# Dividing the first batch's heads by their row sums after the value product

## The chip, the core and the metric

The kernel runs on one core of a Trainium2 chip. The core has five engines with queues of their own: PE (matrix products, out of SBUF into the eight banks of PSUM), DVE and ACT (elementwise work, both read PSUM), POOL (elementwise work on SBUF alone) and SP (which issues the DMAs here). They meet only through semaphores. The metric is the time of one execution in device microseconds, as the median of several; the profile shows one such execution.

## The reference

Three layers stand behind one another: causal attention with a decay bias, a gated MLP, and a routed mixture of experts. The change touches only the end of the attention:

```
scores = scale * q @ k.T                       # 4 batches, 8 heads, 576 tokens, head_dim 64
scores = where(causal, -1e9, scores + minimum(bias, 0))
attn   = exp(scores - max(scores, axis=-1))
attn   = attn / (sum(attn, axis=-1) + 1e-9)    # row sums, one for each query
out    = attn @ v                              # what the MLP and the experts read
```

The division may stand before the product with v, on 576 x 576 exponentials of a head, or behind it, on 576 x 64 outputs.

## The kernel before

There are 32 heads (g = 0 to 31), and two heads make a pair. A head is worked in five blocks of query rows (i = 0 to 4: four of 128 rows, one of 64), block i against the 128 (i + 1) keys that the causal mask leaves it. `A_steps` walks heads and blocks in order and holds back what comes behind a block's scores by four blocks, so that the scores of one head are made while the head before it is finished:

- `emit_S(g, i)`: PE multiplies queries and keys into a PSUM bank (through the helper `mm3`, line 711); DVE adds the mask, takes the negated row maximum and writes the scores to the tile E (L409); ACT turns E into exponentials in place and adds up each row into column i of the tile `lsum` (L417). POOL adds 1e-9 (L421), DVE takes the reciprocal (L422), and POOL multiplies the rows of E by it, in place (L425).
- `emit_T(g, i)`: PE transposes E (L443) into a bank, and ACT or DVE copies that to `eta` (blocks 0 and 1) or `etb` (blocks 2 to 4), with keys on the partitions (L448, L450).
- `emit_PV(g, u)`: PE multiplies the values with `eta` (u = 0, 256 queries) or `etb` (u = 1, 320 queries) (L475). The output has head_dim on 64 partitions and the queries along the columns. ACT copies it to the tile `XF` of the pair (L487).
- `emit_X(p)`: PE transposes `XF` of a finished pair for a store (L504), and POOL splits it in two parts for the MLP (L498, L499).

The first batch (g < F4 = 8) uses plain float32 for exponentials and values; a float32 product stands in the trace as two instructions. In its time nothing of the MLP can run on PE yet. What runs beside it are the preparation of the MLP's weights (`split_f64`, lines 593 to 600, on ACT, DVE and POOL), the cumulated bias (`emit_cum`, lines 226 to 235, on DVE), the transposes of queries and keys for later heads (L334 on PE; lines 340 to 344 on ACT and DVE), and `warm_up` products, which compute nothing that is used (L166). The later batches run side by side with the MLP of the batch ahead of them.

PSUM has seven banks in rotation for all of this (`ps`, in the program's order), so a bank is free again when the engine that reads it has done so. A scheduler sets the order of the instructions on each engine; every engine then works strictly through its queue. Queries and keys of a head are put together by DMAs (`prep_asm`) from a single tile `tst`, which is written anew for the next pair.

Of the kernel before, what the change touches and what calls it, by code (L numbers as in the profile page):

```python
# [13 lines left out]
ALU = mybir.AluOpType  # L14
# [10 lines left out]
def f32v(ap):  # L25
    return ap.bitcast(F32)
# [7 lines left out]
def kernel(  # L34
# [19 lines left out]
    PE, ACT, DVE, POOL, SP = nc.tensor, nc.scalar, nc.vector, nc.gpsimd, nc.sync  # L54
# [7 lines left out]
    NQ = (S + 127) // 128  # L62
    QM = [min(128, S - 128 * i) for i in range(NQ)]
# [31 lines left out]
    def ps(tag="ps", bufs=7):  # L95
        t = psum.tile([128, 512], F32, tag=tag, name=tag, bufs=bufs)
        return t
# [18 lines left out]
    def T(pool, shape, dt, tag, bufs=1):  # L116
        _n[0] += 1
        return pool.tile(shape, dt, tag=tag, name=f"{tag}_{_n[0]}", bufs=bufs)

    ident = T(const, [128, 128], F32, "ident")  # L120
# [266 lines left out]
    Et, lsum, hred = {}, {}, {}  # L387

    def emit_S(g, i):
        qk = QK[buf[g]] if g >= ND else None  # L390
        M = QM[i]
        N = 128 * i + M
        e = T(ap_, [128, 128 * (i + 1)], F32, f"E{i}", bufs=2 if i==0 else 1) if i < NQ - 1 else E4
        Et[g, i] = e
        nm = T(ap_, [128, 2], F32, "negm", bufs=6)
        halves = [(0, N)] if N <= 512 else [(0, HS), (HS, N)]
        for hi, (a, z) in enumerate(halves):
            pt = ps()
            n = z - a
            qs = slice(128 * i, 128 * i + M)  # L400
            if g < ND:
                t = Tst[g // 2][64 * (g % 2):64 * (g % 2) + 64]
                r = slice(32 * g, 32 * g + 2 * NQ)
                pairs = [(t[:, 0, qs], t[:, 1, a:z]), (t[:, 0, qs], t[:, 3, a:z]), (t[:, 2, qs], t[:, 1, a:z]), (sel[r, qs], cumr[r, a:z])]
            else:
                pairs = [(qk[:, 0, qs], qk[:, 1, a:z]), (qk[0:KX, 2, qs], qk[0:KX, 3, a:z])]
            mm3(pt[0:M, 0:n], pairs, True, True)
            m0 = 512 - 128 * i + a if z == N else 0
            hred[g] = DVE.tensor_tensor_reduce(  # L409
                out=e[0:M, a:z], in0=pt[0:M, 0:n], in1=zmask[0:M, m0:m0 + n], scale=-1.0,  # L410
                scalar=BIG if hi == 0 else nm[0:M, 0:1], op0=ALU.add, op1=ALU.min, accum_out=nm[0:M, hi:hi + 1],
            )
        last = len(halves) - 1
        if i == 0:
            lsum[g] = T(ap_, [128, 8], F32, "lsum", bufs=3)
        l = lsum[g]
        ACT.activation(out=e[0:M, 0:N], in_=e[0:M, 0:N], func=ACTF.Exp, scale=-1.0, bias=nm[0:M, last:last + 1], accum_out=l[0:M, i:i + 1])  # L417
        if i in LG:
            i0 = LG[i]
            c = slice(i0, i + 1)  # L420
            POOL.tensor_scalar(out=l[0:M, c], in0=l[0:M, c], scalar1=1e-9, scalar2=0.0, op0=ALU.add, op1=ALU.add)  # L421
            DVE.reciprocal(out=l[0:M, c], in_=l[0:M, c])  # L422
            for x in range(i0, i + 1):
                n = 128 * x + M
                POOL.tensor_scalar(out=Et[g, x][0:M, 0:n], in0=Et[g, x][0:M, 0:n], scalar1=l[0:M, x:x + 1], scalar2=1.0, op0=ALU.mult, op1=ALU.mult)  # L425

    ET = {}
    LG = {z: z for z in range(NQ)}
# [26 lines left out]
    XH, XL, XF = {}, {}, {}  # L455

    def emit_PV(g, u):
        p, r = divmod(g, 2)
        vv = VV[g]
        et = ET.pop((g, u))  # L460
        q0, n = ((0, QA), (QA, QB))[u]
        pt = ps()
        js = range(2) if u == 0 else range(NQ)
        wide = g >= X3
        for j in js:
            kk = 128
            a = max(0, 128 * j - q0)
            if g < F4:
                ms = [(f32v(vv[0:kk, j, 0, :]), 0)]
            elif wide:  # L470
                ms = [(vv[0:kk, j, :, :].rearrange("p a d -> p (a d)"), z) for z in range(2)]
            else:
                ms = [(vv[0:kk, j, 0, :], 0), (vv[0:kk, j, 0, :], 1), (vv[0:kk, j, 1, :], 0)]
            for n_, (l, z) in enumerate(ms):
                PE.matmul(  # L475
                    pt[0:128 if wide else 64, a:n], lhsT=l, rhs=et[0:kk, z, j, a:n] if g >= F4 else f32v(et[0:kk, 0, j, a:n]),
                    start=(j == 0 and n_ == 0), stop=(j == js[-1] and n_ == len(ms) - 1),
                )
        if r == 0 and u == 0:
            XF[p] = T(ap_, [128, S], F32, "xf", bufs=2)  # L480
        po = 64 * r
        if wide:
            xc = T(ap_, [128, QB], F32, "xc")
            ACT.copy(out=xc[po:po + 64, 0:n], in_=pt[64:128, 0:n])
            DVE.tensor_tensor(out=XF[p][po:po + 64, q0:q0 + n], in0=pt[0:64, 0:n], in1=xc[po:po + 64, 0:n], op=ALU.add)
        else:
            ACT.copy(out=XF[p][po:po + 64, q0:q0 + n], in_=pt[0:64, 0:n])  # L487

    X3 = 12
    F4, TA = 8, (1, 3)  # L490
# [29 lines left out]
    def A_steps(LAG):  # L520
        fifo = []
        for n in range(NH * NQ):
            g, i = n // NQ, n % NQ
            p = g // 2
            if i == 0:
                for x in when:
                    if when[x] == g and g:
                        prep_asm(x)
            if g < len(WU) and WU[g]:
                warm_up(WU[g])  # L530
            emit_S(g, i)
            if (g, i) == EC0:
                emit_cum()
            yield 2 * max(107, (128 * i + QM[i]) * 0.42)
            fifo.append((g, i))
            if (g, i) == RS:
                prep_T(1, 0)
                prep_T(1, 1)
                prep_load(2)
                for x in when:  # L540
                    if when[x] == 0:
                        prep_asm(x)
            for p in range(1, NH // 2):
                if (when.get(2 * p) or g) - 1 == g and i in (3, 4):
                    prep_T(p, i - 3)
                    if i == 4 and p + 1 < NH // 2:
                        prep_load(p + 1)
                    yield 600
            if len(fifo) > LAG:
                yield from after(*fifo.pop(0))  # L550
        for x in fifo:
            yield from after(*x)
        emit_PV(NH - 1, 1)
        yield 1230
        emit_X(NH // 2 - 1)
# [6 lines left out]
    def after(g, i):  # L562
        emit_T(g, i)
        yield 110 * (i + 1)
        if i == 2:
            emit_PV(g, 0)
            yield 860
        if i == 1 and g > 0:
            emit_PV(g - 1, 1)
            yield 1230  # L570
        if i == XI and g > 0 and g % 2 == 0:
            emit_X((g - 1) // 2)
            done_x[0] += 1
            yield 600
        if i == 1 and g + 2 < NH:
            prep_V(g + 2)
# [132 lines left out]
    def mm3(pt, pairs, first_, last_):  # L709
        n = len(pairs)  # L710
        ms = [PE.matmul(pt, lhsT=l, rhs=r, start=(first_ and x == 0), stop=(last_ and x == n - 1)) for x, (l, r) in enumerate(pairs)]  # L711
        return ms
# [415 lines left out]
    def fetch(dst, idx, n=NT):  # L1128
        return POOL.indirect_dma_start(
            out=dst, out_offset=None, in_=x2_d[0:n, :], in_offset=bass.IndirectOffsetOnAxis(ap=idx, axis=0),  # L1130
            bounds_check=n - 1, oob_is_err=False,
        )
# [294 lines left out]
    x = fetch(early["xg2"], ids[:, CAP - 1:CAP])  # L1427
# [36 lines left out]
```

## Time and profile before

| what | value |
|---|---|
| median of three runs | 814.5 us (813.86 to 816.91) |
| the profiled execution: its own time | 817.79 us |
| the profiled execution: its span, first to last instruction | 816.0 us |
| busy, share of the span: PE / DVE / ACT / POOL | 95% / 66% / 55% / 42% |
| granted PE clock, mean over the span | 0.962 |

PE is busy nearly all the time, but its busy time holds stretches at half clock, and the ends of its products are modelled. So a share of the whole span says little about one stage: the first batch's heads lie between about 16 and 117 us of the span, and that stage is read by itself. In lists of instructions, a line gives the start, the duration, the engine, the kernel's line, the operation, what it writes and reads, a count and, in brackets, how long the engine stood idle just before and who ended that. "PEld" is the loading of weights into PE, "PEclk" the granted clock, where 1.00 is 2.4 GHz and 0.50 is 1.2 GHz.

### The profile page before, as it was taken

Reading aid. Unit: us, or ns where it says so; the run is one execution under the profiler, and the core shown is the slowest. Engines: PE = TensorE matmul, PEld = TensorE weight load, DVE = VectorE, ACT = ScalarE, POOL = GpSimd, SP = SyncE. Lnnn points to the kernel's source line nnn. Section 1 sums busy time; section 2 is a strip of 40 time slices with the busy share of each in tenths; the row PEclk is TensorE's granted clock in tenths of the full one; section 3 lists DMA queues with packets and bytes.
Section 4 is the critical chain, followed back from the end, with each engine's and each line's share of the span. In section 5 each row is a group of like instructions: output and inputs, shape, how many; then the busy total and the mean of one; then the engine's idle time right before and its main releaser. Section 6 shows DMA issues by size and latency. Waiting matters only on the chain. (4 is left out here: it accounts for less than half of the span.)

```text
span 816.0 us, 14956 instructions
## 1 busy us (share of the span) xinstructions
PE 778.6 (95%) x4744; PEld 652.2 (80%) x4744; DVE 539.1 (66%) x1620; ACT 445.2 (55%) x1073; POOL 343.8 (42%) x625
## 2 busy tenths in 40 slices
PE   9988879898999999999999899998999999999995
PEld 4555559787998888988988778877898988988984
DVE  6389756877666979886888747778455544645630
ACT  4367667677553679762778523613454444545540
POOL 4287762766644348871558610203402131231110
PEclk9599998899899999999999999999999999999998
DMA  6789699986456967766945177312556564565520
GB/s 142 181 186 266 190 199 276 287 187 178 102 128 158 270 160 196 167 148 193 246 99 176 43 231 248 126 40 83 202 176 178 170 197 137 165 199 182 182 80 25
DMA packets 119604, 138.69 MB, mean 170 GB/s; under 512 B 69494, under 2 KB 82934, under 8 KB 119524
## 3 DMA queue, kind: packets, MB, share of 16 engines
q1 hardware_dynamic: 116196, 128.23, 59.4%
q0 software_dynamic: 3328, 9.48, 3.1%
q8 instruction: 39, 0.64, 0.3%
q14 instruction: 41, 0.34, 0.1%
HBM read 89.97 MB, written 22.15 MB: 137 GB/s over the span
## 5 line engine op out<-in xcount | busy, mean ns | idle before, releaser
L1116 DVE TENSOR_TENSOR wp<-wraw,wp 128x1024 fp32r<-128x1024 f32 x63 | 76.8, 1227 | 90.8 <-ACT wp L1115 90.5
L425 POOL TENSOR_SCALAR E<-E,lsum 128x128 f32<-128x128 f32 (+4 forms) x160 | 97.7, 613 | 39.2 <-DVE lsum L422 24.2
L417 ACT ACTIVATE E<-E,negm 128x128 f32<-128x128 f32 (+4 forms) x160 | 96.8, 606 | 24.6 <-DVE negm L409 20.0
L711 PE MATMUL ps<-qk 128*128 128x128 f32 (+4 forms) x372 | 92.7, 347 | 8.6 <-DMA qk<-tst 4.4
L1115 ACT CAST wp<-wraw 128x1024 fp32r<-128x1024 f32 x64 | 66.6, 1049 | 62.1 <-DMA wraw<-in_moe_w_dram 58.0
L711 PE MATMUL ps<-xT,wp 128*128 128x288 f32 (+4 forms) x672 | 99.3, 308 | 0.0
L711 PEld LDWEIGHTS ps<-xT,wp 128*128 128x128 f32 x672 | 98.2, 188 | 0.8
L711 PE MATMUL ps<-wp,hT 128*128 128x512 f32 (+1 forms) x408 | 96.4, 394 | 0.0
L409 DVE CUSTOM_DVE_ANT_0 E<-ps,zmask 128x128 f32<-128x128 f32 (+4 forms) x160 | 75.3, 475 | 31.7 <-PE ps L711 30.7
L421 POOL TENSOR_SCALAR lsum<-lsum 128x1 f32<-128x1 f32 (+1 forms) x160 | 39.9, 249 | 118.4 <-ACT E L417 109.2
L711 PEld LDWEIGHTS ps<-wp,hT 128*128 128x128 f32 (+1 forms) x408 | 75.3, 186 | 17.3
L443 PE MATMUL ps<-ident,E 128*128 128x128 f32 (+1 forms) x480 | 77.9, 271 | 7.2 <-POOL E L425 3.2
L1190 POOL DMA_INDIRECT out_dram<-y,idsr x16 | 20.4, 1274 | 148.5 <-ACT y L1189 115.8
L711 PE MATMUL ps<-wsg,vg 128*128 128x288 f32 x448 | 70.5, 308 | 2.3 <-DVE etb L453 1.0
L711 PEld LDWEIGHTS ps<-qk 128*128 128x128 f32 (+2 forms) x372 | 56.5, 182 | 19.2 <-issue 6.5
L443 PEld LDWEIGHTS ps<-ident,E 128*128 128x128 f32 (+1 forms) x480 | 53.0, 144 | 21.5 <-POOL E L425 7.1
L711 PEld LDWEIGHTS ps<-wsg,vg 128*128 128x128 f32 x448 | 63.6, 194 | 4.1 <-DVE etb L453 1.3
L475 PE MATMUL ps<-etb,vv 128*128 128x320 f32 (+5 forms) x340 | 63.7, 339 | 0.0
L475 PEld LDWEIGHTS ps<-etb,vv 128*128 128x128 f32 (+1 forms) x340 | 50.4, 182 | 12.6 <-issue 4.9
L711 PE MATMUL ps<-xh,w 128*128 128x288 f32 x256 | 58.3, 306 | 0.0
L711 PE MATMUL ps<-w,vg 128*128 128x512 f32 (+1 forms) x216 | 54.6, 397 | 0.1
L711 PE MATMUL ps<-w,xh 128*128 128x512 f32 (+1 forms) x160 | 52.4, 406 | 0.7 <-DVE etb L453 0.7
(316 smaller groups left out, 1582.7 us busy)
## 6 DMA issues: line engine op xcount, KB each, us to landing
wraw<-in_moe_w_dram SPq DMA_DIRECT2D x64, 512.0 KB
qk<-tst SPq DMA_DIRECT2D x28, 432.0 KB
w<-wv_d SPq DMA_DIRECT2D x16, 512.0 KB
w<-wo_d SPq DMA_DIRECT2D x16, 512.0 KB
qk<-tst SPq DMA_DIRECT2D x28, 288.0 KB
w<-wu_d SPq DMA_DIRECT2D x12, 512.0 KB
nq<-in_q_dram SPq DMA_DIRECT2D x32, 144.0 KB
nk<-in_k_dram SPq DMA_DIRECT2D x32, 144.0 KB
```

Source lines behind the costliest of these rows:

```text
L409: hred[g] = DVE.tensor_tensor_reduce(out=e[0:M, a:z], in0=pt[0:M, 0:n], in1=zmask[0:M, m0:m0 + n], scale=-1.0, scalar=BIG if hi == 0 else ...
L417: ACT.activation(out=e[0:M, 0:N], in_=e[0:M, 0:N], func=ACTF.Exp, scale=-1.0, bias=nm[0:M, last:last + 1], accum_out=l[0:M, i:i + 1])
L421: POOL.tensor_scalar(out=l[0:M, c], in0=l[0:M, c], scalar1=1e-9, scalar2=0.0, op0=ALU.add, op1=ALU.add)
L425: POOL.tensor_scalar(out=Et[g, x][0:M, 0:n], in0=Et[g, x][0:M, 0:n], scalar1=l[0:M, x:x + 1], scalar2=1.0, op0=ALU.mult, op1=ALU.mult)
L443: PE.transpose(pt[:, j * M:(j + 1) * M], e[0:M, 128 * j:128 * (j + 1)], ident[0:M, 0:M])
L475: PE.matmul(pt[0:128 if wide else 64, a:n], lhsT=l, rhs=et[0:kk, z, j, a:n] if g >= F4 else f32v(et[0:kk, 0, j, a:n]), start=(j == 0 and n ...
L711: ms = [PE.matmul(pt, lhsT=l, rhs=r, start=(first_ and x == 0), stop=(last_ and x == n - 1)) for x, (l, r) in enumerate(pairs)]
L1115: c = ACT.copy(out=w[:, 0, :], in_=r)
L1116: a = (POOL if (e, j) == (0, KD) else DVE).tensor_tensor(out=w[:, 1, :], in0=r, in1=f32v(w[:, 0, :]), op=ALU.subtract)
L1190: POOL.indirect_dma_start(out=of[:, :], out_offset=bass.IndirectOffsetOnAxis(ap=idx[0:n], axis=0), in_=y[0:n], in_offset=None, bounds_chec ...
```

## The change

For the heads of the first batch POOL no longer scales E. Exponentials go unscaled through the transposes and the product with v. POOL fills `lsum` with ones at the start of a head (columns or rows that no block writes stay 1), adds 1e-9 to two or three columns at once, and DVE takes their reciprocals, twice for a head and not five times. Behind each value product PE makes a second one into a further bank: the weights are one column of reciprocals repeated 128 times, the moving matrix is the identity, and the result is a bank in which every partition holds the reciprocals along the columns. DVE multiplies `XF` by it, in place.

```
@@ emit_S
         if i == 0:
             lsum[g] = T(ap_, [128, 8], F32, "lsum", bufs=3)
+            if g < F4:
+                POOL.memset(lsum[g], 1.0)
...
-        if i in LG:
+        if g < F4:
+            if i in (1, NQ - 1):
+                c = slice(0, 2) if i == 1 else slice(2, NQ)
+                POOL.tensor_scalar(out=l[:, c], in0=l[:, c], scalar1=1e-9, scalar2=0.0, op0=ALU.add, op1=ALU.add)
+                DVE.reciprocal(out=l[:, c], in_=l[:, c])
+        elif i in LG:
@@ emit_PV
             ACT.copy(out=XF[p][po:po + 64, q0:q0 + n], in_=pt[0:64, 0:n])
+        if g < F4:
+
+            pn = ps()
+            for i in range(2) if u == 0 else range(2, NQ):
+                a, M = 128 * i - q0, QM[i]
+                PE.matmul(pn[:, a:a + M], lhsT=lsum[g][:, i:i + 1].to_broadcast([128, 128]), rhs=ident[:, 0:M], start=True, stop=True)
+            x = XF[p][po:po + 64, q0:q0 + n]
+            DVE.tensor_tensor(out=x, in0=pn[po:po + 64, 0:n], in1=x, op=ALU.mult)
```

The scheduler moves some instructions with it. On PE, head 0 and the first blocks of head 1, in the kernel before (E is the block that is transposed, `warm` the operand of the warm-up products, `qk` and `wsg` hold queries, keys and bias):

```order
L711 MATMUL ps<-wsg_143 128x256
L166 LDWEIGHTS warm_107
L166 MATMUL rt<-warm_107 32x512
L166 LDWEIGHTS warm_107
L166 MATMUL rt<-warm_107 32x512
L443 MATMUL ps<-ident_72,E_60_295 128x128 x3
L475 MATMUL ps<-eta_383,vv_219 64x256
L475 MATMUL ps<-eta_383,vv_219 64x128
L711 MATMUL ps<-qk_30_102 128x384 x3
```

And the same place on PE in the changed kernel, whose lines 450, 482, 500 and 726 are the transposes, the value product, the new product and `mm3`:

```order
L726 MATMUL ps<-wsg_143 128x256
L450 MATMUL ps<-ident_72,E_60_292 128x128 x3
L166 LDWEIGHTS warm_107
L166 MATMUL rt<-warm_107 32x512
L166 LDWEIGHTS warm_107
L166 MATMUL rt<-warm_107 32x512
L482 MATMUL ps<-eta_373,vv_219 64x256
L482 MATMUL ps<-eta_373,vv_219 64x128
L500 MATMUL ps<-ident_72,lsum_236 128x128 x2
L726 MATMUL ps<-qk_30_102 128x384 x3
```

The two warm-up products went from ahead of the three transposes to behind them, and two of the new products stand between the value product and the next scores. At the end of head 0 three new products stand behind its second value product, again with two warm-up products beside it.

On POOL, heads 1 and 2 in the kernel before (`vg` is a tile of the weights' preparation, `vt` holds the values' last rows):

```order
L376 TENSOR_SCALAR vv_427<-vt_105 128x64
L598 TENSOR_TENSOR vg_414<-vg_414,g_77_416 128x512
L598 TENSOR_TENSOR vg_574<-vg_574,g_97_576 128x512
L425 TENSOR_SCALAR E_32_104<-E_32_104,lsum_398 64x576
L421 TENSOR_SCALAR lsum_568<-lsum_568 128x1
L425 TENSOR_SCALAR E_92_562<-E_92_562,lsum_568 128x128
L421 TENSOR_SCALAR lsum_568<-lsum_568 128x1 x2
L425 TENSOR_SCALAR E_102_610<-E_102_610,lsum_568 128x256
```

And on POOL at the same place in the changed kernel:

```order
L376 TENSOR_SCALAR vv_415<-vt_105 128x64
L417 MEMSET lsum_682 128x8
L613 TENSOR_TENSOR vg_402<-vg_402,g_77_404 128x512
L613 TENSOR_TENSOR vg_556<-vg_556,g_97_558 128x512
L423 TENSOR_SCALAR lsum_552<-lsum_552 128x2
L376 TENSOR_SCALAR vv_591<-vt_105 128x64
L423 TENSOR_SCALAR lsum_552<-lsum_552 128x3
L417 MEMSET lsum_852 128x8
```

The scalings of E are gone from behind the preparation of weights, and a fill of the next head's `lsum` (the tile of head 3, then that of head 4) stands in the queue instead.

## Rows read from the trace of the kernel before

**Rows 1.** Windows by stage: length; PE, PEld, DVE, ACT, POOL busy (count); PEclk, DMA, GB/s

```profile
16.00:41.00 25.00, 24.89 (x84) 13.16 (x84) 10.13 (x45) 9.64 (x28) 6.98 (x19) 0.57 0.83 186
41.00:55.00 14.00, 12.40 (x60) 7.52 (x60) 11.03 (x35) 9.07 (x25) 10.71 (x19) 0.91 0.79 181
55.00:87.00 32.00, 26.82 (x146) 17.37 (x145) 31.51 (x87) 22.98 (x61) 25.09 (x37) 0.91 1.00 252
87.00:101.00 14.00, 14.00 (x86) 9.98 (x85) 9.66 (x40) 9.94 (x29) 11.14 (x23) 0.97 0.64 169
101.00:117.00 16.00, 14.59 (x96) 10.88 (x96) 10.94 (x43) 11.21 (x37) 10.92 (x28) 1.00 0.98 186
```

**Rows 2.** Instructions of PE in order of time, and one weight load: waits before them

```profile
20.60 0.18 PEld L443 LDWEIGHTS ps<-ident,E 128*128 128x128 f32 x1 [0.84 <-POOL E L425]
...
48.70 0.52 PE L443 MATMUL ps<-ident,E 64*128 64x64 f32 x5 [0.56 <-POOL E L425]
51.47 0.44 PE L443 MATMUL ps<-ident,E 128*128 128x128 f32 x2 [0.97 <-POOL E L425]
68.43 0.52 PE L443 MATMUL ps<-ident,E 64*128 64x64 f32 x5 [1.38 <-POOL E L425]
...
84.12 0.44 PE L711 MATMUL ps<-wsg 128*128 128x128 f32 x2 [1.66 <-DVE negm L409]
...
122.45 0.66 PE L711 MATMUL ps<-qk 128*128 128x128 f32 x2 [3.71 <-DMA qk<-tst]
```

**Rows 3.** PE in order of time: prices of products, each group up to the next start

```profile
93.43 2.27 PE L475 MATMUL ps<-etb,vv 128*64 128x320 f32 x10
95.63 0.51 PE L711 MATMUL ps<-qk 128*128 128x256 f32 x2
...
216.35 1.09 PE L672 MATMUL ps<-idr,w 128*128 128x128 f32 x8
217.27 1.01 PE L663 MATMUL ps<-gl,g 128*128 128x9 f32 x8
218.13 1.04 PE L711 MATMUL ps<-wsg,vg 128*128 128x288 f32 x6
```

**Rows 4.** Groups of instructions by line, 0 to 170 us: busy us, mean ns

```profile
L425 POOL TENSOR_SCALAR E<-E,lsum 128x128 f32<-128x128 f32 (+4 forms) x62 | 39.6, 642 | 12.5 <-DVE lsum L422 9.8 <-PE ps L443 0.4 <-DMA wo_d<-vg 0.3
L421 POOL TENSOR_SCALAR lsum<-lsum 128x1 f32<-128x1 f32 (+1 forms) x62 | 18.1, 292 | 39.4 <-ACT E L417 36.4
```

**Rows 5.** Groups on DVE over the whole span, shapes kept apart: busy us, mean ns

```profile
L422 DVE RECIPROCAL lsum<-lsum 128x1 f32<-128x1 f32 x128 | 19.3, 154 | 14.9 <-POOL lsum L421 14.1
L485 DVE TENSOR_TENSOR xf<-ps,xc 64x320 f32<-64x320 f32 x20 | 9.6, 482 | 3.6 <-ACT xc L484 3.0
L485 DVE TENSOR_TENSOR xf<-ps,xc 64x256 f32<-64x256 f32 x20 | 8.3, 414 | 0.9 <-ACT xc L484 0.7
```

**Rows 6.** Windows of one microsecond in which the clock rises, falls and rises

```profile
43.00:44.00 1.00, 1.00 (x4) 0.40 (x4) 1.00 (x2) 0.00 (x0) 0.00 (x0) 0.72 0.92 187
70.00:71.00 1.00, 0.67 (x6) 0.33 (x4) 0.95 (x8) 0.00 (x0) 0.76 (x3) 0.94 1.14 177
74.00:75.00 1.00, 1.00 (x6) 0.63 (x5) 0.99 (x3) 0.09 (x1) 0.68 (x2) 0.86 1.06 362
```

**Rows 7.** PE in order of time at half clock, head 0

```profile
24.30 1.03 PE L166 MATMUL rt<-warm 128*32 128x512 bf16 x2
25.26 0.90 PE L443 MATMUL ps<-ident,E 128*128 128x128 f32 x3
26.10 1.54 PE L475 MATMUL ps<-eta,vv 128*64 128x256 f32 x4
27.57 1.33 PE L711 MATMUL ps<-qk 64*128 64x384 f32 x3
...
40.17 1.04 PE L166 MATMUL rt<-warm 128*32 128x512 bf16 x2
41.13 3.45 PE L475 MATMUL ps<-etb,vv 128*64 128x320 f32 x10
```

## The prediction

> **What bounds the kernel now.** I read the windows by stage first. PE carries the time almost everywhere, so the question is what PE does while the first batch's heads are worked, from 16 to 117 us. The windows show four different limits [rows 1]. From 16 to 41 us PE is busy 24.89 of 25 us, but at a mean clock of 0.57: it is bound by itself, at half speed. From 41 to 55 us it is idle 1.6 us. From 55 to 87 us it is idle 5.18 of 32 us, while DVE is busy 31.51: here DVE's queue leads. From 87 to 101 us PE is busy 14.00 of 14 us at nearly full clock. From 101 to 117 us it is idle 1.41 us.
>
> Then I read who ends PE's waits. The scaling of E on POOL, which the change removes, ended four that matter, of 0.84, 0.56, 0.97 and 1.38 us, each in front of transposes [rows 2]. That is all the direct return there is: 0.84 in the first stage, 1.53 in the second, 1.38 in the third. POOL's own load (62 scalings of 642 ns and 62 small additions of 292 ns [rows 4], of which this change takes the 40 of the first batch, 37 us in all) is no bound of the span and returns nothing by itself.
>
> Last I looked at the clock. It is at half from about 20 us to 43.5 us (which the mean of 0.57 from 16 to 41 us [rows 1] and 0.72 at 43 us [rows 6] give), and again from 70.9 to 74.3 us, just after the 1.38 us wait (0.94 at 70 us, 0.86 at 74 us [rows 6]). The first stretch is the largest loss of the stage.
>
> **The change part by part.**
>
> *New products on PE.* Five for a head, four of 128 columns and one of 64, in plain float32, so 40 products as 80 instructions. The trace has no such product with full-width weights and 128 float32 columns, so I bound it. The value product of one head, ten instructions over 2 x 1216 columns, advances 2.20 us from 93.43 to 95.63 [rows 3], or 0.905 ns a column and instruction: two instructions of 128 columns then cost 0.23 us, 8.3 us in all (4608 columns). That has narrower weights. Eight full-width loads with only nine columns advance 0.86 us, 0.107 each [rows 3]; if nothing of a load lay under its columns, an instruction would cost 0.107 + 0.116 us and all of them about 17 us. But eight pairs of a full-width load and a single pass of 128 columns (L672) advance 0.92 us, 0.115 each [rows 3], hardly more than the load alone, so loads and columns do overlap. I take 0.13 us an instruction, 0.26 us a product (nearest to that row), 10.1 us in all.
>
> *Where they fall.* A: two before 41 us, at half clock, so 0.96 us. B: ten between 41 and 55 us, 2.6 us. C: thirteen between 55 and 87 us, 3.4 us. D: seven between 87 and 101 us, 1.8 us. E: eight behind that, 2.1 us.
>
> A: 0.96 less the wait of 0.84 is +0.1 us. B: 2.6 less 1.53 is +1.1 us.
>
> C: the wait of 1.38 goes, and with it, since PE no longer stands idle just ahead of it, the half-clock stretch at 70.9 us, 3.4 us long and so 1.7 us lost. Of the idle time that is left (5.18 - 1.38 = 3.8 us) I let the new products fill half, 1.9 us. 3.4 - 1.38 - 1.7 - 1.9 = -1.6 us. The ends: +2.0 us if only POOL's wait returns, -3.5 us if the products vanish wholly in the idle time. D: PE has no slack, +1.8 us in full.
>
> E: hidden. Queries and keys for the head behind come by a DMA for which PE waits 3.71 us at 122.45 [rows 2]. The chain that leads there starts with the end of an earlier head's scores, at about 100 us, so eight products behind that (2.1 us) fall into this wait. Without that cover they would cost 2.1 us.
>
> *DVE.* A head loses five reciprocals of 154 ns and gains two, and two multiplications out of PSUM like those of L485 (414 and 482 ns [rows 5]): +0.4 us a head, inside C some 1.3 us, and elsewhere beside idle time of DVE (in D it is busy 9.66 of 14 us). Each multiplication waits for the new product and for ACT's copy; behind it in DVE's queue stand row maxima of the next block, whose scores come behind that product on PE anyway. The lost half of the idle time in C is meant to hold this.
>
> *POOL and ACT.* Two additions and a fill for a head are left. The fill is a new wait: the exponentials of a head's first block wait for the fill of `lsum`, which stands behind the values' copy and the weights' preparation in POOL's queue. It is due some ten us after what it waits for, so I cost it at nothing; were it late, ACT's queue would stop for up to one preparation. `emit_X` reads `XF` one multiplication later (0.48 us), which the MLP's start does not feel, since it comes behind PE's own transposes. No DMA is added.
>
> *The clock.* Sum so far: 0.1 + 1.1 - 1.6 + 1.8 = +1.4 us. What raises the clock is seen in rows 7: PE is busy without a break from 20 us on, with transposes and narrow score products between short value products, and the clock stays at half; it rises only in a run of two warm-up products and a whole float32 value product, from 40.17 to 44.5 us. The change makes such a run earlier: in the new order the two warm-up products stand directly ahead of the first value product, and two float32 products directly behind it, where before three transposes parted them (25.26, 26.10 and 27.57 [rows 7]). The run holds eight float32 instructions and the later one ten, which are longer, so I do not take the rise at its end (about 28 us) as given, and not at the old place either; I take the middle, 35.8 us. 7.75 us of half-clock work then shrink to 3.9, and with the 11% of idle time that PE has in B at full clock, to 4.3: -3.4 us.
>
> The Trainium skill (TensorE: Matmul & The Clock Gate, Part 4: PE-mode transpose) says that transposes do not count as activity in the way other products do. The trace agrees as far as a busy engine at half clock can show it. By that rule the added plain products would bring the full rise, the first rival below.
>
> **Sum.** +1.4 - 3.4 = -2.0 us. The profiled execution took 817.8 us (span 816.0 and 1.8 around it), 3.3 above the median; its stages are taken to differ from the median's run by nothing that the change touches. So 815.8 against 817.8, and against the median of 814.5: **812.5 us**.
>
> **The rivals.** *The clock rises with the first value product*, at 28 us: 15.5 us of half-clock work shrink to 8.7, -6.8 and not -3.4 us. 814.5 + 1.4 - 6.8 = 809.1 us. For it: the same kinds of instructions stand in the run as in the one that raised it. Against it: eight shorter float32 instructions here, ten there.
>
> *The clock rises where it did*: 814.5 + 1.4 = 815.9 us. For it: one run of value product and scores, 26.10 to 28.9 us, did not raise it.
>
> *Slower: waits change their name.* The banks of the new products come free only when DVE's queue reaches the multiplication, and in C that queue is full (31.51 of 32 us). PE then waits for banks where it waited for POOL (such a wait on DVE already stands at 84.12, 1.66 us [rows 2]), and nothing is returned: 0.96 + 2.6 + 3.4 + 1.8 = 8.8 us, of which the clock may give back 2: 821 us. It decides as soon as fewer than half of those 8.8 us come back.
>
> *The DMA leads*: if the 3.71 us wait at 122.45 ends when it did, whatever PE does before, the whole stage moves nothing: 814.5 us. Against it: the DMAs it waits for are issued only when PE has freed their buffer.
>
> **How the numbers follow.** A measurement of this kernel can tell about 0.5%, 4.1 us, from no change: the bounds are 810.4 and 818.6 us. Chances: forecast 0.30, early rise 0.24, no rise 0.22, slower 0.17, DMA 0.07. Faster: most of the early rise (0.20) and the lower third of the forecast (0.09), 0.29. Slower: 0.15 of the slower rival and 0.04 of the no-rise case with the dear end of the product's price, 0.19. Same: 0.52. The range reaches from 807 us (early rise with all of C's lower end) to 820.5 us (most of the slower rival), and leaves out 0.1 on either side.
>
> **What would show it.** Right: no wait on POOL ahead of the transposes up to 117 us; new products that advance about 0.13 us an instruction at full clock; a clock that is up before 43.5 us and stays up at 71 us; from 87 to 101 us a stage that is longer by about 1.8 us; a shorter wait at the DMA near 122 us. Wrong: waits on DVE that grow between 55 and 87 us, new products of 0.2 us an instruction, or a new half-clock stretch.

## The result

The kernel after took 819.2 us (median of 20 executions, 813.3 to 824.4) beside 813.3 for the kernel before (20 executions, 804.6 to 816.9): a ratio of 1.0090, with a 95% interval of 1.0067 to 1.0113. It is 0.9% slower, and the forecast of 812.5 us, 2 us faster, was wrong in its sign. The time itself lies inside the range given (807.0 to 820.5). The ratios, here and below, leave out executions more than 1.5% above the fastest of the same kernel; all other numbers hold every execution.

The profiled execution of after took 820.55 us, with a span of 818.7. Its windows by stage, with the columns of [rows 1]:

```profile
16.00:41.00 25.00, 25.00 (x84) 13.72 (x83) 10.84 (x42) 10.23 (x30) 1.18 (x5) 0.54 0.79 182
41.00:55.00 14.00, 14.00 (x79) 8.91 (x78) 11.32 (x31) 8.89 (x23) 5.33 (x10) 0.96 0.79 185
55.00:87.00 32.00, 28.70 (x168) 20.53 (x167) 29.69 (x81) 22.20 (x59) 14.19 (x17) 0.88 0.86 233
87.00:101.00 14.00, 13.71 (x77) 9.42 (x76) 8.50 (x31) 7.46 (x21) 3.26 (x9) 0.90 0.85 207
101.00:117.00 16.00, 13.70 (x95) 10.69 (x95) 9.15 (x34) 9.42 (x30) 5.68 (x14) 1.00 0.69 154
117.00:129.00 12.00, 12.00 (x75) 9.54 (x75) 7.73 (x33) 7.80 (x25) 8.55 (x19) 0.86 0.79 186
```

POOL's load is gone as intended (14.19 us busy from 55 to 87 us, where it was 25.09). PE is busy all the time up to 55 us, and from 55 to 87 us for 1.9 us more than before. But the clock from 16 to 41 us is 0.54, no higher than in [rows 1], and from 55 to 101 us it is lower than it was.

What PE waited for from 16 to 130 us, in the view of waits of after (total, times, longest):

```profile
PE ps L450 <- DVE lsum L429: 2.2, 1, 2.2
PE ps L334 <- DVE xf L502: 1.9, 1, 1.9
PE ps L482 <- DVE etb L457: 1.4, 2, 1.1
```

In before, PE's waits on POOL are this row of the same view, 0.56, 0.97, 0.33 and 1.38 us:

```profile
PE ps L443 <- POOL E L425: 3.2, 4, 1.4
```

They are gone, and so are the 1.66 us on DVE and the 3.71 us for queries and keys. Waits on DVE, in three rows, stand in their place. The second is the bank wait that the prediction's slower rival described: the multiplication (L502) that frees a bank comes only at 78.62 us. The first is another thing, and no step of the prediction had it.

The new products themselves cost what was foreseen. In the list of PE's instructions of after, two groups of them, each up to the next start:

```profile
46.05 0.71 PE L500 MATMUL ps<-ident,lsum 128*128 128x128 f32 x4
46.52 0.60 PE L726 MATMUL ps<-qk 128*128 128x384 f32 x2
...
53.23 0.88 PE L500 MATMUL ps<-ident,lsum 128*128 128x128 f32 x6
53.91 0.49 PE L726 MATMUL ps<-wsg 128*128 128x256 f32 x2
```

0.47 us for four and 0.68 for six (two of them with 64 columns) are 0.117 and 0.113 us an instruction, where 0.13 was taken: 9.2 us for all 80 at full clock.

### The profile page after: what moved, and what is told of

Same layout as the page of the kernel before. It is cut to its first block, busy times and chain, and to the rows that moved or that the text cites. A ratio compares the mean times of both kernels' runs of the same rounds, so it can differ in the third digit from the quotient of the medians.

```text
span 818.7 us, 15025 instructions
## 1 busy us (share of the span) xinstructions
PE 784.7 (96%) x4824; PEld 659.4 (81%) x4824; DVE 541.9 (66%) x1612; ACT 444.3 (54%) x1073; POOL 310.4 (38%) x569
## 5 line engine op out<-in xcount | busy, mean ns | idle before, releaser
L432 POOL TENSOR_SCALAR E<-E,lsum 64x576 f32<-64x576 f32 (+4 forms) x120 | 71.6, 598 | 34.7 <-DVE lsum L429 23.1
L428 POOL TENSOR_SCALAR lsum<-lsum 128x1 f32<-128x1 f32 (+1 forms) x120 | 27.3, 227 | 98.7 <-ACT E L419 88.4
```

## The experiments

**How they are compared.** The time of one kernel differs from execution to execution by up to 20 us, and it follows the mean granted clock of that execution: the kernel before took 804.4 us at 0.977 and 819.9 at 0.958. So two numbers are given for each run. One is the median with the ratio to the kernel before. The other is the difference from before at the same mean clock (0.967): the 237 executions of the thirteen kernels that stay within 2% of before were fitted with one level for each kernel and one common slope, which is -0.59 us for each 0.001 of clock; the scatter round the lines is 1.6 us, and ± is a 95% interval. A difference at the same clock leaves out what a change does to the clock; the median holds both.

Each edit also makes the scheduler set a new order. By the order of instructions in the traces, the kernels of the table differ from the ones that they were made from in dozens of places on DVE alone, with two exceptions: e13 (from after) and e15 (from e10) keep every order on PE, ACT and POOL, and on DVE only the moved instruction and a few of its neighbours change places. So these two compare one thing; each of the others compares its edit together with a new order.

| kernel | median, us (executions) | ratio to before, 95% interval | mean clock | at the same clock, us |
|---|---|---|---|---|
| before | 813.2 (103) | 1 | 0.967 | 0 |
| after | 819.2 (20) | 1.0090, 1.0067 to 1.0113 | 0.966 | +5.4 ± 0.8 |
| e1, before + unread products | 821.9 (6) | 1.0142, 1.0085 to 1.0199 | 0.966 | +8.3 ± 1.3 |
| e2, before without division | 810.2 (12) | 0.9971, 0.9933 to 1.0009 | 0.970 | -1.9 ± 0.9 |
| e4, after without multiplying | 820.7 (6) | 1.0105, 1.0046 to 1.0163 | 0.967 | +5.4 ± 1.3 |
| e6, after, multiplying by one | 813.8 (12) | 0.9981, 0.9943 to 1.0018 | 0.965 | -2.4 ± 0.9 |
| e7, after, products twice | 825.9 (6) | 1.0158, 1.0113 to 1.0204 | 0.971 | +13.8 ± 1.3 |
| e8, after, more warm-ups | 819.4 (12) | 1.0093, 1.0051 to 1.0135 | 0.967 | +8.0 ± 0.9 |
| e10, heads 6 and 7 alone | 816.7 (12) | 1.0023, 0.9980 to 1.0065 | 0.967 | +1.7 ± 0.9 |
| e11, heads 0 to 3 alone | 814.1 (12) | 1.0024, 0.9989 to 1.0059 | 0.969 | +1.9 ± 0.9 |
| e13, after, bbc halved late | 813.5 (12) | 0.9996, 0.9962 to 1.0029 | 0.971 | +2.5 ± 0.9 |
| e14, before, bbc halved late | 813.7 (12) | 0.9998, 0.9955 to 1.0042 | 0.968 | +1.4 ± 0.9 |
| e15, heads 6 and 7, bbc late | 812.9 (12) | 0.9986, 0.9949 to 1.0023 | 0.969 | -0.5 ± 0.9 |

Theory A, formed on after's trace, was that PE's queue is the bound and is longer by the products. Theory B was that the division at the output is late in itself, since DVE's multiplication holds a bank.

**e1: the products alone.** They are added to the kernel before, with a column of the identity as weights, and nothing reads them.

```
+        if g < F4:
+            pn = ps()
+            for i in range(2) if u == 0 else range(2, NQ):
+                a, M = 128 * i - q0, QM[i]
+                PE.matmul(pn[:, a:a + M], lhsT=ident[:, i:i + 1].to_broadcast([128, 128]), rhs=ident[:, 0:M], ...)
```

> The kernel before, with the forty new products added behind the value products, with weights that are a column of the identity and not of reciprocals; nothing reads their bank, and POOL's scaling of E stays. The changed kernel's trace has these products at 0.117 us an instruction at full clock, 9.2 us for the eighth heads together. Theory A (the change is slower because PE's queue is longer by the products): plus 5 to 9 us on the kernel before, as the 3.7 us wait for a DMA near 122 us hides about two of them. Theory B (the products fit in PE's idle time, and the loss is the multiplication that holds their bank in DVE's queue): plus 0 to 3 us.

Measured: +8.3 us at the same clock, nearly all of the 9.2 us that they take; the wait for the DMA is 2.7 us there, 1 us shorter. This is theory A's result.

**e2: no division.** The kernel before, with the first batch not divided at all (no additions, reciprocals or scalings there).

```
-        if i in LG:
+        if i in LG and g >= F4:
```

> The kernel before, where the first batch's heads are not divided at all: no additions and scalings on POOL, no reciprocals on DVE, nothing in their place. This is what the change takes away, by itself. Both theories: a gain, 3 to 4 us by the waits on POOL in the trace of before (0.84, 0.56, 0.97 and 1.38 us), up to 8 us if the half-clock stretches behind them go as well. If the gain is under 1.5 us, POOL's scaling was off the path and the change had nothing to win.

Measured: -1.9 us, less than the 3 to 4 expected. So the removal of POOL's scaling returns about 1.9 us. The view of waits of e2, PE from 16 to 130 us, shows where the rest went:

```profile
PE ps L475 <- DVE etb L450: 2.2, 1, 2.2
PE ps L711 <- DVE negm L409: 2.0, 3, 0.7
PE ps L711 <- DMA qk<-tst: 1.8, 2, 1.6
PE ps L443 <- DVE eta L450: 1.0, 1, 1.0
```

No wait on POOL is left, but the waits on DVE, which is next in the chain, grew from 3.7 us in before (1.8 on `negm`, 1.2 on `etb`, 0.7 on `tst`) to 6.1 (5.2 in these rows). The first of them, 2.2 us, ends at 68.12 us, where before waits for POOL, and a half-clock stretch follows it as it does there, from 68.9 to 72.3 us. One of its windows:

```profile
70.00:71.00 1.00, 1.00 (x4) 0.54 (x3) 0.97 (x2) 0.69 (x2) 0.00 (x0) 0.50 1.05 284
```

**e3: a constant for the products.** After, with the multiplication by a constant -0.5 in place of the products.

```
-            DVE.tensor_tensor(out=x, in0=pn[po:po + 64, 0:n], in1=x, op=ALU.mult)
+            DVE.tensor_tensor(out=x, in0=mhalf[po:po + 64, 0:1].to_broadcast([64, n]), in1=x, op=ALU.mult)
```

> The changed kernel without its forty products: DVE multiplies the output by a constant out of SBUF (-0.5) in place of the bank of reciprocals, so the division is left out, but the multiplications, the fills, the additions and the reciprocals stay. Theory A: 6 to 9 us under the changed kernel, so 0 to 3 us under the kernel before. Theory B: also under the changed kernel, since no bank waits for the multiplication, but by 3 to 6 us; it does not tell the two apart by itself, only with the next one.

Measured: 848.8 us, which says nothing on the question. The factor turned the first batch's attention round, the routing of tokens to experts came out another way, and the experts' overflow pass ran at the end of the program, which no other kernel here did. e6 asks the same with a factor of one.

**e4: the products stay, the multiplication goes.** The first batch is not divided.

```
-            x = XF[p][po:po + 64, q0:q0 + n]
-            DVE.tensor_tensor(out=x, in0=pn[po:po + 64, 0:n], in1=x, op=ALU.mult)
```

> The changed kernel with its forty products, but DVE does not multiply by them: the bank is free as soon as PE has written it, and the division is left out. Theory A: within 2 us of the changed kernel. Theory B: 4 to 7 us under it, about the kernel before; PE's wait of 1.90 us for the multiplication at 79 us and the half-clock stretch behind it (80 to 90 us) are then gone.

Measured: +5.4 ± 1.3 us, the same as after. The bank wait of 1.9 us is gone from its trace, and nothing came back: theory B falls. A half-clock stretch stands there all the same, from 75.9 to 82.7 us.

**e6: the multiplication stays, the products go.** The first batch is not divided.

```
-            pn = ps() ... PE.matmul(pn[:, a:a + M], ...)
-            DVE.tensor_tensor(out=x, in0=pn[po:po + 64, 0:n], in1=x, op=ALU.mult)
+            DVE.tensor_tensor(out=x, in0=mone[po:po + 64, 0:1].to_broadcast([64, n]), in1=x, op=ALU.mult)
```

> The kernel after without its products: VectorE multiplies by a constant one in place of the spread reciprocals (the first batch is not divided). Fills of lsum, sums, reciprocals and multiplications all stay. Theory A: near the run without any division, 809 to 813 (its 810.2 plus what the multiplications add to VectorE's queue, 0.9 us a head beside other work). Theory B (multiplications and fills are the loss): 816 to 820, as after.

Measured: -2.4 us, as without any division. Fills, sums, reciprocals and multiplications together cost nothing that can be measured.

**e7: each product twice.**

```
+                for _ in range(2):
                     PE.matmul(pn[:, a:a + M], lhsT=lsum[g][:, i:i + 1].to_broadcast([128, 128]), rhs=ident[:, 0:M], ...)
```

> The kernel after with each of the 40 products issued twice into the same bank, 80 more PE instructions. Theory A (each instruction adds its 0.115 us to a queue that has no room): 9 us above after, 826 to 830. Theory B (the loss of after is a wait or a held bank, and the products lie in the queue's gaps): 819 to 822. Between the two (some of the first set hid in gaps that the second set no longer finds): the second set costs more than the first did.

Measured: 8.4 ± 1.5 us over after at the same clock: the second set costs no less than the first (7.7 ± 1.1, after against e6). Theory A again.

**e8: the clock term by itself.**

```
-    WU = (2, 2, 2)
+    WU = (4, 2, 2)
```

> The kernel after with four instead of two warm-ups before each of the five score blocks of head 0: 10 more PE instructions. It measures the clock term of the prediction: if PE's work in head 0 decides when the clock rises, the stretch from 16 to 41 us shows a granted clock of 0.8 or more in the profile and the median falls by some 3 us less the 10 warm-ups' own time of 2 us at full clock: 816 to 819. If the rise doesn't hang on this, the stretch stays near 0.55 and the time grows by the warm-ups at half clock, about 4 us: 821 to 824.

Measured: the median of after, 819.4, between the two forecasts. The profile does show the early rise, as its first two windows say:

```profile
16.00:41.00 25.00, 25.00 (x119) 14.47 (x118) 14.84 (x53) 13.09 (x37) 5.85 (x9) 0.86 0.95 213
41.00:55.00 14.00, 14.00 (x88) 9.20 (x86) 11.12 (x31) 10.05 (x27) 6.25 (x10) 1.00 0.98 234
```

But over all 12 executions the mean clock is only 0.0012 above after's, worth 0.7 us by the slope, and the warm-ups cost 2.7 ± 1.2 us at the same clock. In the profiled executions of e1, e4 and e7 the clock rose early too (0.86, 0.80 and 0.80 in the first window); in those of before, after, e2, e6, e10, e11, e13, e14 and e15 it did not (0.53 to 0.59). One profile of a kernel can't say how often it comes. The mean clocks can say something: the four executions had 0.972 to 0.977, the nine others 0.956 to 0.971, and executions at 0.972 or more are 29 of before's 103 and 1 of after's 20. So it seems to come in single executions of the kernel before too, and there is no sign that the change made it more frequent. It carried the median neither of after nor of e8.

**e5, e9 and e12: the same division without the products.** e6 leaves room for a version some 2 us below before. Three ways to spread the sums or reciprocals without PE were tried; all are far slower. In e5, columns of ones beside the values let the value product put the sums on 64 more partitions:

```
+            POOL.memset(f32v(vv[:, :, 1, :]), 1.0)
...
+            ACT.copy(out=xc[po:po + 64, 0:n], in_=pt[64:128, 0:n])
+            DVE.reciprocal(out=xc[po:po + 64, 0:n], in_=xc[po:po + 64, 0:n])
+            POOL.tensor_tensor(out=x, in0=xc[po:po + 64, 0:n], in1=x, op=ALU.mult)
```

> The same idea with no product added: a column block of ones beside each head's values (64 wide) lets the value product itself put the row sums on 64 more partitions of its bank; ScalarE copies both halves out, VectorE takes reciprocals, POOL multiplies. Theory A (PE's queue is the bound and the 80 product instructions are the loss): PE's count is that of the kernel before, POOL's waits before the transposes are gone as in the run without any division (810.2 median beside 813.3 before), so 808 to 813, about 3 below before and 9 below after. Theory B (division at the output is late in itself: it holds banks and lengthens VectorE's queue): VectorE's and ScalarE's extra work, about 0.9 us a head on each, is there all the same, so 816 to 820. Theory C (what POOL's scaling gave PE was never time, only a place where PE rested): no gain over before, 812.5 to 815.

Measured: 839.2 us (ratio 1.0342, 1.0291 to 1.0392). Groups by line and shape, 16 to 157 us (count, total, mean ns):

```profile
L492 DVE RECIPROCAL xc<-xc 64x320 f32<-64x320 f32 x8 | 17.1, 2143 | 0.1
L492 DVE RECIPROCAL xc<-xc 64x256 f32<-64x256 f32 x8 | 13.9, 1743 | 0.1
...
L451 DVE COPY etb<-ps 128x384 f32<-128x384 f32 x8 | 4.3, 533 | 0.5 <-PE ps L444 0.5
L451 DVE COPY etb<-ps 128x320 f32<-128x320 f32 x8 | 3.9, 482 | 1.2 <-PE ps L444 1.2
```

64 more columns cost the reciprocal 400 ns, or 6.3 a column, and the copy 51 ns, 0.8 a column. No theory had these 31 us of reciprocals on DVE: the trace of before only has reciprocals of one column (154 ns [rows 5]). From 16 to 130 us POOL's multiplication waits 44.5 us for them, and PE 10.0 us for POOL's result, so they are the likely loss; no run takes them out by themselves. The Trainium skill (VectorE: DVE Perf Modes, First, the fixed hardware budget) says that the reciprocal is an iterative division with a repeat count of 8. The ratio of 6.3 to 0.8 agrees.

In e9 the five reciprocals of a head go to a row in DRAM and come back spread over 64 partitions, and DVE multiplies a pair at once.

```
+            dma(linv_d[g].rearrange("(i p) -> p i", p=128), lsum[g][:, 0:NQ])      # emit_T(g, 4)
+            dma(f32v(XL[p][po:po + 64, :]), linv_d[g:g + 1, 0:S].to_broadcast([64, S]))   # emit_PV(g, 1)
+            DVE.tensor_tensor(out=xf, in0=xf, in1=f32v(xl), op=ALU.mult)           # emit_X(p)
```

> Division at the output with PE left out: the five reciprocals of a head go to a DRAM row by one DMA (640 elements of 4 bytes), come back spread over 64 partitions by a second (147 KB), and VectorE multiplies a whole pair (128x576) once, just before the pair is transposed. 16 DMAs and 4 multiplications in place of 80 PE instructions and 16 multiplications. Theory A (the products on PE are the loss): the level of the run with the multiplication by a constant one, which lies about 2 us under before at the same mean clock (810.3 beside 812.5), so 809.5 to 813, if the 1.2 MB that are moved more hide. Theory B (in this stretch transfers are the next bound): the added 1.2 MB take some 6 us of a stream that moved 186 to 252 GB/s there, and the times come to 814 to 819.

Measured: 865.1 us (1.0609, 1.0562 to 1.0656). What stands out in the trace is neither theory's, but SP's own queue, 16 to 220 us:

```profile
SPq L78 <- DMA linv_d<-lsum: 42.8, 7, 9.4
```

SP stands for 42.8 us behind the write of the row, with every later load behind it. In e12 POOL's queue issues the write, and the reads of a pair stand half a head later.

> The same division by two DMAs a head, with the queue's wait taken away: in the run before this one SyncE's queue stood 42.8 us in 7 waits for the row to land before it could issue the read, with every later load behind it. Now POOL's own queue issues the write right behind the reciprocals, and SyncE's reads of a pair stand half a head later, before the third block of the next pair is transposed. Theory A (the products on PE are the loss, and the transfers hide): the level of the multiplication by a constant one, some 2 us under before at the same mean clock, 809.5 to 813. Theory B (a round trip through DRAM cannot be hidden in this stretch, by the queue or by the 1.2 MB that it adds): above before, 815 or more.

Measured: 846.7 us (1.0470, 1.0411 to 1.0529), 18 us under e9 but above before, as theory B has it: the write of 640 elements of 4 bytes takes 9.0 to 10.7 us from issue to landing, SP still waits 25.0 us for it, and POOL 21.5 us for the tile that it reads.

**e10 and e11: which heads cost.**

```
-            if g < F4:                       # three places
+            if 6 <= g < F4:                  # e10; in e11: if g < 4
```

> The change for heads 6 and 7 alone (20 product instructions); heads 0 to 5 are scaled by POOL as before. The prediction held that these products hide in the 3.71 us in which PE waits for a transfer after head 7. If so, no more than 0.5 us over before at the same mean clock. If every product counts alike, a quarter of after's 5.6 us: 1.4 us over before.

> The change for heads 0 to 3 alone (40 product instructions), heads 4 to 7 as before. If every product counts alike, half of after's 5.6 us: 2.8 us over before at the same mean clock. If the products of heads 6 and 7 are hidden, heads 0 to 5 carry it all, and these four some 3.7. If the release of POOL in these heads pays for them, as the prediction held for heads 2 to 4 (a gain of 1.6 beside losses of 0.1 and 1.1), about 0.4 or less.

Measured: +1.7 and +1.9 us at the same clock. Heads 6 and 7, whose products were to be hidden, cost as much as four early heads. Each is ± 0.9: the first fits an equal price for every product (1.4); the second lies between its three figures and leaves out 0.4 and 3.7. The waits of PE in e10 have the row of after again, and none on a transfer:

```profile
PE ps L450 <- POOL E L432: 3.3, 4, 1.4
PE ps L450 <- DVE lsum L429: 2.2, 1, 2.2
```

**The wait that takes the place of the hidden one.** In after, DVE and PE in order of time:

```profile
111.98 0.08 DVE L409 DVE_READ_ACCUMULATOR2_ANT negm<- 128x1 f32 x1
114.69 0.46 DVE L1361 TENSOR_SCALAR bbc<-bbc 128x576 f32<-128x576 f32 x1 [2.63 <-DMA bbc<-in_moe_b_sg_dram]
115.07 0.48 DVE L457 COPY etb<-ps 128x320 f32<-128x320 f32 x1
115.47 0.15 DVE L429 RECIPROCAL lsum<-lsum 128x1 f32<-128x1 f32 x1
...
115.70 0.30 PE L450 MATMUL ps<-ident,E 128*128 128x128 f32 x1 [2.24 <-DVE lsum L429]
```

`bbc` is a bias of the MLP's gate, loaded by a DMA that SP issues at 110.42 us and halved by DVE at a place in its queue that the scheduler sets. Nothing reads `bbc` before 209 us, but what stands behind it is needed at once: the copy of head 7's last block and a reciprocal of head 8. In the kernel before SP issues that load at 106.4 us, and the halving stands later in head 8, behind the split of queries and keys, where it waits for nothing:

```profile
111.25 0.43 DVE L341 SCALAR_TENSOR_TENSOR tst<-ps,tst 128x288 fp32r<-128x288 f32 x1
111.61 0.44 DVE L344 TENSOR_TENSOR tst<-ps,tst 128x288 fp32r<-128x288 f32 x1
112.05 0.46 DVE L1346 TENSOR_SCALAR bbc<-bbc 128x576 f32<-128x576 f32 x1
112.43 0.62 DVE L453 TENSOR_TENSOR eta<-ps,eta 128x128 fp32r<-128x128 f32 x2
```

e13, e14 and e15 move that one instruction behind head 10's scores, in after, in before and in e10; PE's order in e13 is that of after, and in e15 that of e10, instruction by instruction.

```
-        DVE.tensor_scalar(out=bbc, in0=bbc, scalar1=0.5, scalar2=None, op0=ALU.mult)
+        behind(DVE.tensor_scalar(out=bbc, in0=bbc, scalar1=0.5, scalar2=None, op0=ALU.mult), hred[10].ins.name)
```

> The kernel after with one VectorE instruction moved: the halving of bbc stands behind the scores of head 10. PE's order is that of after. Theory D (the wait behind bbc's load takes up what the transfer wait was to cover): the 2.24 us wait on lsum is gone and the time falls by 1.5 to 2.2 us against after at the same mean clock, from 5.5 to some 3.5 over before. Theory A (each product adds its own time wherever PE waits): the wait goes, another one comes in its place, and the time stays within 0.7 us of after.

> The control: the kernel before with the same move. Nothing on PE waits for bbc's load there except 0.72 us, behind which 3.71 us for a transfer follow. Both theories: within 0.7 us of before. A gain of over 1 us here would make any gain of the other two runs one of the move and not of the change.

> Heads 6 and 7 alone divided at the output, with the halving of bbc behind head 10's scores. Theory D: the products hide, 0 to 0.5 us over before at the same mean clock in place of 1.8. Theory A: 1.4 to 1.8 us over before as without the move.

Measured: e13 takes 813.5 us, the median of before (ratio 0.9996, 0.9962 to 1.0029; the interval lies wholly below after's); at the same clock it is 2.8 ± 1.2 us under after and still 2.5 ± 0.9 over before. e15 falls from 816.7 to 812.9, and at the same clock from +1.7 to -0.5. Both falls are at least as large as theory D said and leave out theory A's. The control e14 gains nothing, but it is a poorer control than was meant: the scheduler set a new order on all four engines there, and at the same clock it is 1.4 ± 0.9 over before, where 0.7 at most was expected. (Its 0.72 us wait is still there, so that wait was not bbc's.) Theory D holds by e13 and e15. PE's waits in e13, and its window from 117 to 129 us:

```profile
PE ps L726 <- DMA qk<-tst: 2.6, 1, 2.6
PE ps L334 <- DVE xf L502: 1.6, 1, 1.6
...
117.00:129.00 12.00, 9.45 (x77) 8.67 (x76) 7.09 (x27) 7.71 (x24) 8.47 (x18) 1.00 1.01 238
```

The wait for queries and keys is there again, 2.6 us, shorter than the 3.71 of [rows 2], as the prediction wanted it. And the clock is 1.00 here, where after's is 0.86: the 2.24 us in which PE stood idle were followed in after by a half-clock stretch. Two windows of after, ahead of it and in it:

```profile
116.00:117.00 1.00, 0.95 (x5) 0.67 (x6) 1.00 (x3) 0.33 (x2) 0.59 (x2) 1.00 1.14 247
118.00:119.00 1.00, 1.00 (x3) 0.46 (x2) 0.83 (x4) 0.49 (x4) 0.84 (x3) 0.50 0.54 111
```

So the wait's direct cost at the same clock is 2.8 ± 1.2 us (e13 against after), as large as the wait; another 2.7 us of the medians' 5.7 lie in the mean clock (0.9708 against 0.9662, by the slope). That the clock's whole difference comes from this one stretch is not shown: it stands from 117.2 to 120.6 us and loses 1.7.

## Why the prediction was wrong

The sum as measured, at the same clock: -2.4 us for POOL's release with all of DVE's new work (e6), +4.9 ± 1.3 for the products (e13 against e6), +2.8 for the wait behind `bbc`, together after's +5.4. The three are differences along one chain of kernels, so they add up by construction; only the last comes from a comparison in which almost nothing else moved. The forecast had +1.4 at the same clock, and -2.0 with its clock term. Three of its terms failed, each by about 3 us (the release, the cover in E, the clock), and the products came out 2 us cheaper than their terms. Step by step:

- **The products.** Their price held (9.2 us against 10.1 taken; the two of A, at half clock, took 1.16 us against 0.96). Without a new wait about 5 us of them remain in the time, where the terms of A to D leave 6.9 (8.8 less the 1.9 of idle time that they were to fill in C). Added to a kernel that has no release to offer (e1) or a second time (e7), they cost 8.3 and 8.4; why they cost more there is not shown.
- **What the release returns.** This term was too large. A, B and C counted 0.84, 1.53 and 1.38 us of waits and 1.7 of clock, 5.45 us in all. The whole release is worth 1.9 to 2.4 us (e2, e6). The 0.84 us was misread: it is idle time of the weight loads, while PE is busy for 24.89 of the 25 us [rows 1]. PE's own waits on POOL are 3.2 us in all. For the rest, the prediction asked what is late next only for bank and DMA; in e2 it is DVE, at `etb`, `negm` and `eta`, and the half-clock stretch of C, which was to go with POOL's wait, follows DVE's wait instead. In after that stretch went, as said, but behind the bank wait at 77.3 us another stands, from 79.6 to 89.9, three times as long.
- **D** held: from the value product of head 5 at 96.37 to that of head 6 at 104.92 us after takes 8.55 us, where before takes 7.43 (93.43 to 100.86): 1.12 us for five products, and no slack.
- **E, hidden.** The mechanism fits the runs in which it could act (e15: -0.5 us, and the wait at the DMA is 1.5 us there and 2.6 in e13, where before has 3.7), but in after it did not act: DVE's queue stopped 2.6 us for an unrelated load ahead of it, and the cover was spent. Of the failed steps, this is the one whose cause a run shows by itself. The prediction read the order on PE and the length of the waits, and said of DVE only that its work elsewhere lies beside idle time. It didn't ask where, in the new order, DVE's own waits for loads stand.
- **DVE's additions and the fill** cost nothing that can be measured, as costed (e4, e6).
- **The clock term, -3.4 us.** Not there: after's mean clock is 0.9662 and before's 0.9672. The early rise did come in the profiled executions of e1, e4, e7 and e8, but not in after's; what decides it is open. The Trainium skill (TensorE: Matmul & The Clock Gate, Part 4: PE-mode transpose) says that transposes do not count as activity in the way other products do; the full rise that the prediction's first rival drew from it did not come in after.

Of the rivals, "waits change their name" came nearest in time (821 against 819.2) and in kind, since idle time was not returned but passed on. Its mechanism is not the cause: without the multiplication that holds the banks the time is the same (e4), and PE's waits on DVE from 55 to 87 us are 3.0 us before and after. No version that divides measurably beats the kernel before: e15 equals it, e13 has its median but lies 2.5 ± 0.9 us over it at the same clock, and even a free spreading (e6) would save about 2 us.

## What to carry to other kernels

Taking away an engine's work returns at most what a run without that work shows, and not the sum of the waits that it ended: here (e2) PE's waits on POOL of 3.2 us went, those on DVE grew by 2.4, and 1.9 us were returned. When a change makes a scheduler set a new order, look in every queue for instructions that wait for a load which nobody needs yet, and at what stands behind them: one such instruction decided here between a median of 819.2 and one of 813.5 us. Where times follow the granted clock, compare executions at the same clock before a difference under 1% is explained.

## What the runs showed of the hardware

- The time follows the mean granted clock within one kernel, 0.59 us for each 0.001, over 20 us in all; the executions of the kernel before had mean clocks from 0.954 to 0.986.
- DVE's reciprocal costs 6.3 ns a column (1743 ns for 256, 2143 for 320), some eight times a copy's 0.8 (e5).
- A DMA that scatters 640 elements of 4 bytes into a row of DRAM lands 9.0 to 10.7 us after its issue (e12).
